# A dynamic convolution with a gated feed-forward behind it: the shifted copy of x by a second transposing DMA, scales from sums of magnitudes, and a written order for six blocks

## The chip, the cores and the metric

The kernel runs on one core of a Trainium2 chip. The metric is the time of one execution on the device in microseconds; below, "us" is always that. TensorE does the matmuls, VectorE, ScalarE and GpSimd work on tiles element by element, and the queue of SyncE issues nearly all DMAs.

## What is computed

For each of 16384 tokens (4 sequences of 4096) the reference mixes the last seven rows of x, with a softmax over seven numbers per head as weights, and puts the result through a normalised, gated feed-forward.

```python
w = softmax(weight_gen, axis=-1)                     # 8 heads, 7 taps
out = einsum('bshk,bskhg->bshg', w, x_unf)           # x_unf: the last 7 rows of x, 8 heads of 24
x = out.reshape(B * S, 192)
xn = x / sqrt(mean(x * x) + 1e-06) * rms_g
g = xn @ w_gate                                      # 192 x 1536
val = xn @ w_val
return (g * sigmoid(g) * val) @ w_out                # 1536 x 192
```

x, weight_gen and rms_g are 32-bit; the three weight matrices come as 64-bit numbers.

## The kernel before

**Blocks and stages.** A block is 512 tokens; there are 32. For each block VectorE (with TensorE for blocks 0 and 1) forms the seven taps, ScalarE and GpSimd make the factor of the norm, and the result is split in two 16-bit halves, high and low, in the tile sp. A transposing DMA turns sp into tt, with the 192 features on the partitions. Stage 1 (s1_mm) multiplies by w_gate and w_val in 12 chunks of 128 hidden columns: nine pairs of matmuls a chunk, gate on 64 partitions and value on the other 64, which run side by side. Each pair wants some 64-row groups of x on the upper and some on the lower half of the partitions, so there is a second tile tu, which is tt with its two halves swapped (PLACE says which group lies where). Products of high and low halves are summed in a bank of PSUM. s1_evac takes the two banks out (silu on ScalarE, the product on VectorE), s1_split makes the 16-bit halves of the hidden values (tile hh), stage 2 (s2_mm) multiplies by w_out and s2_evac writes the result out.

**Transposes.** The function trans issues three DMAs on SyncE's queue: the transpose sp to tt, and two copies of 64 partitions from tt to tu, which wait for the transpose to land. The same queue issues the loads of x and the weights and the writes of the result.

**Weights.** The 64-bit words of w_gate and w_val come in four slices (SL) of 2, 3, 3 and 4 chunks, loaded by load_gate_val with one DMA for the gate, to 64 partitions, and one for the value, to the other 64. decode turns them in place into 32-bit numbers (two steps on ScalarE, two on VectorE). A scale, a power of two, is found for each column and slice: ScalarE squares the slice (square_slice, tile sq), TensorE sums the squares (L524), VectorE copies the sums (L530), TensorE sums them again (L533, L538) and VectorE takes the root by arithmetic on the exponent (scales). Then high_gate_val and low_gate_val write the 16-bit halves in wm. w_out goes the same way (square_out, scale_out, tile wost). Slices 2 and 3 are kept in rawb, one of the two buffers that hold hh later.

**The order.** For blocks 0 to 3 (FRONT = 4) the order of the instructions on all five engines is written out by hand: each letter of the string START advances one stream of work by a step. W is a matmul on zeros that keeps TensorE at work (heat), A, B, C, c, D and G are the convolutions of blocks 0 to 5, s the scales, t and T the high and low halves of wm, S stage 1 in order of blocks 0 to 3, E and F its two evacuation steps, H and L the split, O stage 2. From block 4 on a planner lays the pairs of blocks out: 24 chunks of stage 1, then 24 steps of stage 2, with the convolutions of the next two blocks between them by cost.

Of the kernel before, what the change touches and what calls it, by code (L numbers as in the profile page):

```python
# [19 lines left out]
P = 128  # L20
R = 16
# [5 lines left out]
LOADS = ("w0", "x0", "s0", "w1", "x1", "s1", "s2", "s3", "x2", "wo", "w2", "x3", "x4")  # L27
START = (
    "M.....aaaa..a.aWWWWWWWWWWWWWWWWWWAAAdd!AAAb1bAbb1bd1AAAAbddBsgAB1AsBAAAAAWgsAAttjjWWgBgj"
    "gsABBjstBmmjTTTssB1mttSStTEBsTBTBmEsF1SmSBEttBFstTSBsBETTFHBHBEBs.Lt.BtSCFFBtuSTSETTHEEu"  # L30
    "L.FHSSSFECuLBLHvSvEHFFLuESSCvFEHuESFSCvLEvCFLCCyEHSEHLLyFHCHHSFyFLEzZSFEzzzCHzzSzLCZEEzF"
    "ZLZCCZSZZZzzHzLZEHSCCSEzZZOCZLCHFCCOOCOOFO3PCPECHCCCcLLOOHcQCOOOFOScFFLLPHHHHFQLcQPHESFS"
    "LLc3EFHEHLSSQESL.EEFFHH3LccFccSSS3OOEOcc3cHPO3OEccOLLQLLcDOOFOOOPcOEcSFcQDccccEcDcSHDFSE"
    "LPFDScEDDDFEDFDQHSEHHFDLLHDHFSESPSLLEFFHFLDELGSSS.EDHDEEFFDHGGDDLFSSESHEHSEQLLGLGDFSHGFG"
    "OLOOHGOGDHHHOLPGEOLFDGFOLGHDGEHOQGFOFOOOOHLHDLLPOPQQLLDPQOODOOOOOGGPGOPQGGPOQGOPGGGGQQG"
# [14 lines left out]
def tile_dynamic_conv_swiglu(  # L50
# [35 lines left out]
    p_h = ctx.enter_context(tc.tile_pool(name="p_h", bufs=2))  # L86
# [8 lines left out]
    def take():  # L95
        return banks[idle.pop(0)]
# [15 lines left out]
    eps = const.tile([P, 1], F32, name="eps")  # L112
# [83 lines left out]
    xsp = {}  # L196

    def conv(i, pe=False):
# [11 lines left out]
        if not pe and i < FRONT + 2:  # L210
# [13 lines left out]
        for k in range(K if pe or i >= FRONT + 2 else 0):  # L224
# [36 lines left out]
        if pe or i < FRONT + 2:  # L261
            sp = p_s.tile([P, J, 2 * D], F16, tag="sp", name="sp", bufs=1)
# [11 lines left out]
            xsp[i] = sp  # L274
# [15 lines left out]
        xsp[i] = sp  # L290

# [3 lines left out]
    def trans(i):  # L295
        sp = xsp.pop(i)
# [620 lines left out]
```

## Time and profile before

| | us |
|---|---|
| three runs | 1169.66, 1170.32, 1170.42; median 1170.32 |
| span of the profiled execution | 1168.1 (its own time is not listed apart) |
| TensorE busy | 1159.1 (99%) |
| VectorE, ScalarE, GpSimd busy | 938.7, 654.9, 556.6 |
| first stage-1 matmul, in the chain that ended last | 35.93 |
| end of the last matmul in that chain | 1164.78 |

The span runs from the first to the last instruction of the profiled execution; the times of the three runs are taken around the whole execution. Matmuls are pipelined, so the busy time of TensorE says that it always had one in work, not that it ran at its peak. A row of a time line gives the start, the time taken, the engine, the line of the kernel, the operation, the tiles written and read and, in brackets, how long the engine stood idle before and what ended that.

### The profile page before, as it was taken

Reading aid. Unit: us, or ns where it says so; the run is one execution under the profiler, and the core shown is the slowest. Engines: PE = TensorE matmul, PEld = TensorE weight load, DVE = VectorE, ACT = ScalarE, POOL = GpSimd, SP = SyncE. Lnnn points to the kernel's source line nnn. Section 1 sums busy time; section 2 is a strip of 40 time slices with the busy share of each in tenths; the row PEclk is TensorE's granted clock in tenths of the full one; section 3 lists DMA queues with packets and bytes.
Section 4 is the critical chain, followed back from the end, with each engine's and each line's share of the span. In section 5 each row is a group of like instructions: output and inputs, shape, how many; then the busy total and the mean of one; then the engine's idle time right before and its main releaser. Section 6 shows DMA issues by size and latency. Waiting matters only on the chain.

```text
span 1168.1 us, 24415 instructions
## 1 busy us (share of the span) xinstructions
PE 1159.1 (99%) x10182; PEld 628.7 (54%) x10183; DVE 938.7 (80%) x1120; ACT 654.9 (56%) x1275; POOL 556.6 (48%) x466
## 2 busy tenths in 40 slices
PE   8999999999999999999999999999999999999998
PEld 4455564564645546465564645546465464645546
DVE  8999976888788887888878898788987888778531
ACT  5986555556365563646636465465645646455462
POOL 1223463626365453645636456353644627355351
PEclk9999999999999999999999999999999999999999
DMA  9603322050110501114030330304102030110300
GB/s 222 182 2 116 118 42 56 1 172 1 42 42 5 168 1 45 39 36 137 2 82 1 66 107 1 82 1 135 39 19 64 2 82 2 41 42 1 82 1 28
DMA packets 67638, 67.34 MB, mean 58 GB/s; under 512 B 52428, under 2 KB 54604, under 8 KB 66632
## 3 DMA queue, kind: packets, MB, share of 16 engines
q1 hardware_dynamic: 67016, 64.77, 20.9%
q8 instruction: 79, 1.29, 0.4%
q10 hardware_dynamic: 480, 1.02, 0.4%
q14 instruction: 31, 0.25, 0.1%
q0 software_dynamic: 32, 0.00, 0.0%
HBM read 28.03 MB, written 12.58 MB: 35 GB/s over the span
## 4 chain that ended last, share of the span: by engine, by line
PE 97%; DMA 2%; ACT 0%; SPq 0%; issue 0%; ACTq 0%
PE bank L350 64%; PE bank L402 21%; PE bank L405 11%; DMA rawb<-in_moe_w_val_dram 2%; DMA rawa<-in_moe_w_gate_dram 1%; PE bank L396 0%; ACT rawb L451 0%; ACT rawb L445 0%; ACT sq L512 0%; PE bank L601 0%; PE bank L524 0%; SPq L489 0%; SPq L146 0%; ACT ot L415 0%; SPq L143 0%
## 5 line engine op out<-in xcount | busy, mean ns | idle before, releaser
L379 POOL TENSOR_TENSOR hh<-hf,hh 128x512 f16<-128x512 f32 x372 | 462.6, 1251 | 312.5 <-ACT hh L377 305.7
L350 PEld LDWEIGHTS <-wm 64*128 64x128 f16 x6912 | 334.7, 94 | 408.2 <-issue 3.8
L350 PE MATMUL bank<-tt,wm 64*128 64x512 f16 x3456 | 476.1, 376 | 0.0
L350 PE MATMUL bank<-tu,wm 64*128 64x512 f16 x3456 | 475.9, 376 | 0.0
L363 ACT ACTIVATE sg<-bank,isc 128x512 f32<-128x512 f32 x384 | 263.4, 686 | 227.9 <-PE bank L350 227.0
L402 PE MATMUL bank<-wo,hh 128*128 128x384 f16 x1524 | 374.9, 326 | 0.0
L405 PE MATMUL bank<-wo,hh 128*128 128x192 f16 x1524 | 373.4, 246 | 0.0
L367 DVE SCALAR_TENSOR_TENSOR hf<-bank,cs,sg 128x512 f32<-128x512 f32 x384 | 283.5, 744 | 111.1 <-ACT sg L363 108.8
L377 ACT ACTIVATE hh<-hf 128x512 f16<-128x512 f32 x384 | 238.1, 623 | 32.7 <-DVE hf L367 32.6
L233 DVE TENSOR_TENSOR taps<-xg,wt 128x768 f32<-128x768 f32 x170 | 233.9, 1379 | 0.0
L247 DVE TENSOR_TENSOR acc<-acc,taps 128x768 f32<-128x768 f32 x156 | 209.8, 1345 | 0.9
L402 PEld LDWEIGHTS <-hh 128*128 128x128 f16 x1524 | 149.1, 98 | 104.7 <-issue 7.2
L405 PEld LDWEIGHTS <-hh 128*128 128x128 f16 x1524 | 149.1, 98 | 0.0
L260 POOL TENSOR_TENSOR rs<-rs,mhalf 128x4 f32<-128x4 f32 x32 | 42.1, 1316 | 187.6 <-DVE rs L256 187.6
L422 DVE SCALAR_TENSOR_TENSOR ot<-bank,so,lo 128x192 f32<-128x192 f32 x127 | 51.8, 408 | 85.4 <-ACT lo L421 85.4
L421 ACT ACTIVATE lo<-bank,so 128x192 f32<-128x192 f32 x127 | 50.3, 411 | 96.4 <-PE bank L405 95.2
L252 ACT ACTIVATE junk<-acc 128x192 bf16<-128x192 f32 x120 | 43.4, 362 | 51.3 <-DVE acc L247 48.8
L287 POOL TENSOR_TENSOR sp<-xn,sp 128x768 f16<-128x768 f32 x26 | 42.8, 1645 | 53.3 <-ACT sp L285 53.3
L285 ACT ACTIVATE sp<-xn 128x768 f16<-128x768 f32 x26 | 22.0, 845 | 76.0 <-DVE xn L278 76.0
L278 DVE TENSOR_TENSOR xn<-acc,rs 128x768 f32<-128x768 f32 x26 | 24.9, 956 | 17.6 <-POOL rs L260 17.6
L233 DVE TENSOR_TENSOR acc<-xg,wt 128x768 f32<-128x768 f32 x26 | 35.4, 1360 | 0.0
L214 DVE TENSOR_TENSOR taps<-xg,wt 128x768 f32<-128x768 f32 x28 | 27.3, 995 | 0.0
(96 smaller groups left out, 304.7 us busy)
## 6 DMA issues: line engine op xcount, KB each, us to landing
tu<-tt SPq DMA_DIRECT2D x64, 192.0 KB, 3.0
out_dram<-ot SPq DMA_DIRECT2D x31, 384.0 KB, 3.0
xg<-in_x_dram SPq DMA_DIRECT2D x7, 1536.0 KB, 8.8
wt<-in_weight_gen_dram SPq DMA_DIRECT2D x7, 448.0 KB, 9.4
wost<-in_moe_w_out_dram SPq DMA_DIRECT2D x1, 2304.0 KB, 10.5
xg<-in_x_dram SPq DMA_DIRECT2D x4, 576.0 KB, 5.4
xg<-in_x_dram SPq DMA_DIRECT2D x3, 504.0 KB, 5.7
xg<-in_x_dram SPq DMA_DIRECT2D x2, 384.0 KB, 6.8
```

The costliest lines, as they stand in the source:

```text
L233: mul = nc.vector.tensor_tensor(out=dst.rearrange("p j (h c) -> p (j h) c", h=H), in0=xk, in1=wk, op=ALU.mult)
L247: yield nc.vector.tensor_tensor(out=acc, in0=acc, in1=dst, op=ALU.add)
L252: yield nc.scalar.activation(out=junk, in_=acc[:, j - a, :], func=AF.Square, accum_out=ssq[:, j : j + 1])
L350: mm = nc.tensor.matmul(pt, wm[h, grp, wpart, f], xT[i][half != m][h, q], start=(n == 0), stop=(n == 8))
L363: gate = nc.scalar.activation(out=sg, in_=pg, func=AF.Silu, scale=isc[:, o : o + 1])
L367: both = nc.vector.scalar_tensor_tensor(out=hf_of[i, c], in0=pv, scalar=cs1[:, c : c + 1], in1=sg, op0=ALU.mult, op1=ALU.mult)
L377: yield nc.scalar.activation(out=hid[i][:, 0, c, :], in_=hf, func=AF.Copy)
L379: yield low.tensor_tensor(out=hid[i][:, 1, c, :], in0=hf, in1=hid[i][:, 0, c, :], op=ALU.subtract)
L402: mm = nc.tensor.matmul(pt[:, 0 : 2 * D], hid[i][:, 0, n, c], wo[:, n, :], start=(n == 0), stop=False,)
L405: nc.tensor.matmul(pt[:, 0:D], hid[i][:, 1, n, c], wo[:, n, 0:D], start=False, stop=(n == NC - 1),)
L421: yield nc.scalar.activation(out=lo, in_=pt[:, D : 2 * D], func=AF.Identity, scale=so[:, 1:2])
L422: nc.vector.scalar_tensor_tensor(out=ot[i][:, t, :], in0=pt[:, 0:D], scalar=so[:, 1:2], in1=lo, op0=ALU.mult, op1=ALU.add,)
```

## The change

- The tile sp becomes a part of a wider tile, spare, with 64 zero columns ahead of it and behind it. trans issues two transposing DMAs from it: tt from the middle part, and tu from the whole tile, which shifts the groups by 64 columns, so that each group lies on the other half of the partitions. tu has 13 blocks where tt has 12. The two copies and PLACE are gone; xpart_of finds a group's place.
- The scales come from sums of magnitudes. After the first of decode's two VectorE steps the lower half of each 64-bit word holds the magnitude; its upper 16 bits, every fourth half word of the tile, are read by TensorE as weights (sizes). The squares on ScalarE are gone, and the first sum is squared when it is taken out (ScalarE, six to eight columns). A small constant (least) is added by one more matmul a chunk.
- Stage 1, stage 2, their evacuations and the split have a stream each for even and for odd blocks, the order is written for blocks 0 to 5, and the string of LOADS and steps is new. hh becomes two fixed tiles, hids, one for even and one for odd blocks. Slice 2 is kept in wo until w_out needs it, slice 3 in the upper half of hids[1]. LOW_BY says for each split of the six blocks whether VectorE ("v") or GpSimd ("p") makes the low half.
- The first load of weight_gen goes by SyncE's queue, and w1 is issued ahead of x0.

```diff
-DECODE = ("aa",) * (3 * NS + 4)
-FRONT = 4
+LOW_BY = "ppppppppppppppvvppvpvvpvpvvpppvppppv", "pppppppppvppvvppvpppppvpvvppppvvvpvp"
+FRONT = 6
+LEAD = 6
...
+    SPAN = J * 6 * L
+    spare = const.tile([P, SPAN + 2 * L], F16, name="spare")
+    spl = spare[:, L : L + SPAN].rearrange("p (j c) -> p j c", j=J)
+    hids = [const.tile([P, NC, 2, TB], F16, name=f"hid{n}") for n in range(2)]
...
-        (nc.scalar if a == g == 0 else nc.sync).dma_start(out=dst[:, a:b, :], in_=src[:, a:b, :])
+        nc.sync.dma_start(out=dst[:, a:b, :], in_=src[:, a:b, :])
...
         tt = p_t.tile([P, J * 3, P], F16, tag="tt", name="tt")
-        nc.sync.dma_start_transpose(out=tt, in_=sp.rearrange("p j c -> p (j c)"))
-        tu = p_t.tile([P, J * 3, P], F16, tag="tu", name="tu")
-        nc.sync.dma_start(out=tu[L:P], in_=tt[0:L])
-        nc.sync.dma_start(out=tu[0:L], in_=tt[L:P])
-        xT[i] = [t.rearrange("p (j q) c -> p q j c", q=3) for t in (tt, tu)]
+        nc.sync.dma_start_transpose(out=tt, in_=spare[:, L : L + SPAN])
+        tu = p_t.tile([P, J * 3 + 1, P], F16, tag="tu", name="tu")
+        nc.sync.dma_start_transpose(out=tu, in_=spare)
+        xT[i] = tt, tu
+
+    def xpart_of(i, h, blk, part):
+        t, u = xT[i]
+        b = 3 * part + blk
+        if b % 2 == h:
+            t, q = t, b // 2
+        else:
+            t, q = u, (b + 1) // 2
+        return t[h * L : (h + 1) * L, q : q + 3 * (J - 1) + 1 : 3, :]
...
-    def square_slice(k):
-        n = (SL[k][1] - SL[k][0]) * P
+    def decode_slice(k):
         yield from decode(raws[k].rearrange("p m f -> p (m f)"), "aa")
-        sqs[k] = p_d.tile([P, 3, 4 * P], BF16, tag="sq", name="sq", bufs=2)
-        whole = upper(raws[k].rearrange("p m f -> p (m f)")).bitcast(F32)
-        yield nc.scalar.activation(
-            out=sqs[k][:, :, 0:n], in_=whole.rearrange("p (m f) -> p m f", m=3), func=AF.Square, bias=eps,
-        )
+
+    def sizes(raw):
+        return raw.bitcast(BF16).rearrange("p (f t) -> p f t", t=4)[:, :, 1]
...
                 nc.tensor.matmul(
-                    pt[:, 3 + 2 * c : 5 + 2 * c], sq[:, m, c * P : (c + 1) * P], g2[:, m, :],
-                    start=(m == 0), stop=(m == 2),
-                )
+                    pt[:, 3 + 2 * c : 5 + 2 * c], sizes(raws[k][:, m, c * P : (c + 1) * P]), g2[:, m, :],
+                    start=(m == 0), stop=False,
+                )
+            nc.tensor.matmul(pt[:, 3 + 2 * c : 5 + 2 * c], ones[0:1, :], least, start=False, stop=True)
...
-        nc.vector.tensor_copy(out=sums[:, 0 : w - 3], in_=pt[:, 3:w])
+        nc.scalar.activation(out=sums[:, 0 : w - 3], in_=pt[:, 3:w], func=AF.Square, scale=2.0**-12)
...
+    half = [[(i, c) for i in range(n, FRONT, 2) for c in range(NC)] for n in range(2)]
+    for n in range(2):
+        streams["SV"[n]] = each((s1_mm, i, c) for i, c in half[n])
+        streams["Oo"[n]] = each((s2_mm, b, *unit(u)) for b in range(n, FRONT, 2) for u in range(NC))
```

How the string moves the instructions on ScalarE, ahead of the first stage-1 evacuation (sg), before: rawb holds slices 2 and 3 (1536 columns are slice 3), sq the squares, junk is block 1's norm.

```order
L445 ACTIVATE rawb<-rawb 128x1152
L451 ACTIVATE rawb<-rawb 128x1152
L512 ACTIVATE sq<-rawa,eps 128x3x384
L562 ACTIVATE wm<-rawa,gs 128x256
L445 ACTIVATE rawb<-rawb 128x1536
L451 ACTIVATE rawb<-rawb 128x1536
L512 ACTIVATE sq<-rawb,eps 128x3x384
L252 ACTIVATE junk,ssq<-bank_93 128x192
L562 ACTIVATE wm<-rawa,gs 128x384 x3
L363 ACT_TABLE_LOAD
```

And the same place on ScalarE with the change: wo holds slice 2, hid slice 3, sums are the squared sums of slices 1 and 2.

```order
L421 ACTIVATE wo<-wo 128x1152
L427 ACTIVATE wo<-wo 128x1152
L492 ACTIVATE sums<-bank_92 128x6
L421 ACTIVATE hid_116<-hid_116 128x1536
L427 ACTIVATE hid_116<-hid_116 128x1536
L492 ACTIVATE sums<-bank_91 128x6
L524 ACTIVATE wm<-rawa,gs 128x256
L524 ACTIVATE wm<-rawa,gs 128x384 x2
L255 ACTIVATE junk,ssq<-bank_89 128x192
L524 ACTIVATE wm<-rawa,gs 128x384
```

The squares are gone, two steps of six columns stand for them, and the two decodes of slice 3 stand ahead of the second of these and of the last high half of slice 0.

On SyncE's queue, from the last two loads of weights on, before: the transposes and copies of blocks 0 and 1, the rest of x (128x1536), w_out and the next weight_gen.

```order
L489 DMA rawb<-in_moe_w_gate_dram 64x3x512
L489 DMA rawb<-in_moe_w_val_dram 64x3x512
L299 DMA_TRANSPOSE tt<-sp 128x12x128
L302 DMA tu<-tt 64x1536
L303 DMA tu<-tt 64x1536
L168 DMA xg<-in_x_dram 128x1536
L578 DMA wost<-in_moe_w_out_dram 128x12x192
L175 DMA wt<-in_weight_gen_dram 128x896
L299 DMA_TRANSPOSE tt<-sp 128x12x128
```

The same place on SyncE's queue with the change, up to block 1's transposes and the loads behind them.

```order
L468 DMA hid_116<-in_moe_w_gate_dram 64x3x512
L468 DMA hid_116<-in_moe_w_val_dram 64x3x512
L298 DMA_TRANSPOSE tt<-spare 128x12x128
L301 DMA_TRANSPOSE tu<-spare 128x13x128
L540 DMA wost<-in_moe_w_out_dram 128x12x192
L298 DMA_TRANSPOSE tt<-spare 128x12x128
L301 DMA_TRANSPOSE tu<-spare 128x13x128
L173 DMA xg<-in_x_dram 128x1536
L180 DMA wt<-in_weight_gen_dram 128x896
```

Each block has two DMAs here in place of three, none of them waits for the one ahead of it to land, and block 1's now stand ahead of the rest of x.

## Rows read from the trace of the kernel before

**Rows 1.** The page: busy time, share of the span and instructions by engine.

```profile
PE 1159.1 (99%) x10182; PEld 628.7 (54%) x10183; DVE 938.7 (80%) x1120; ACT 654.9 (56%) x1275; POOL 556.6 (48%) x466
```

**Rows 2.** Chain that ended last, first 50 us: start, us, what.

```profile
11.62 19.40 DMA rawb<-in_moe_w_val_dram
...
32.67 1.63 ACT rawb L451
34.29 1.22 ACT sq L512
...
35.93 3.99 PE bank L350 x36
...
40.23 3.99 PE bank L350 x36
44.23 0.39 PE bank L524 x12
```

**Rows 3.** The same chain over the whole span.

```profile
68.52 1.17 PE bank L601 x24
...
179.77 46.73 PE bank L350 x432
...
250.12 46.73 PE bank L350 x432
...
1164.78 0.42 ACT ot L415
```

**Rows 4.** Time line of ScalarE (ACT): a step of three columns, slice 3's first decode.

```profile
13.60 0.17 ACT L660 ACTIVATE g_sb<-bank 128x3 f32<-128x3 f32 x1 [0.88 <-PE bank L656]
...
31.11 1.68 ACT L445 ACTIVATE rawb<-rawb 128x1536 f32<-128x1536 f32 x1 [1.05 <-DMA rawb<-in_moe_w_val_dram]
```

**Rows 5.** Time line of TensorE (PE): taps of blocks 0 and 1, heating matmuls.

```profile
13.49 5.43 PE L240 MATMUL bank<-taps,ident 128*128 128x384 f32 x16
...
24.35 0.59 PE L788 MATMUL bank<-dull 128*128 128x512 bf16 x2
27.02 2.93 PE L240 MATMUL bank<-taps,ident 128*128 128x384 f32 x4 [2.08 <-DVE taps L233]
```

**Rows 6.** Groups of TensorE's weight loads (PEld) by form: busy us, mean ns.

```profile
L240 PEld LDWEIGHTS bank<-taps,ident 128*128 128x128 f32 x56 | 10.5, 199 | 11.1 <-DVE taps L233 3.9 <-issue 2.1
```

**Rows 7.** Time line of SyncE's queue (SPq): transposes and first copies, blocks 0 and 1.

```profile
24.89 1.53 SPq L299 DMA_TRANSPOSE tt<-sp  x1
32.52 0.53 SPq L302 DMA_DIRECT2D tu<-tt  x1
...
50.67 1.43 SPq L299 DMA_TRANSPOSE tt<-sp  x1
54.34 0.47 SPq L302 DMA_DIRECT2D tu<-tt  x1
```

**Rows 8.** Stretches of block 1's transpose and copies: busy us by engine, PEclk, DMA share, GB/s.

```profile
51.50:54.00 2.50, 2.50 (x26) 1.17 (x24) 2.50 (x5) 2.50 (x6) 1.29 (x1) 1.00 0.83 157
55.00:57.50 2.50, 2.50 (x26) 1.15 (x24) 2.50 (x4) 2.50 (x4) 0.85 (x1) 1.00 0.63 155
```

**Rows 9.** DMA issues: the row of gains, size, us from issue to landing.

```profile
g_row<-in_moe_rms_g_dram POOLq DMA_DIRECT2D x1, 0.8 KB, 7.0
```

**Rows 10.** Time line of GpSimd (POOL): the issue of that DMA.

```profile
2.14 0.68 POOL L650 DMA_DIRECT2D g_row<-in_moe_rms_g_dram  x1
```

**Rows 11.** Stretches of the start: busy us of PE, PEld, DVE, ACT, POOL, then PEclk.

```profile
25.00:30.00 5.00, 2.98 (x12) 1.47 (x13) 5.00 (x5) 4.46 (x5) 0.00 (x0) 0.70 1.05 205
...
50.00:55.00 5.00, 5.00 (x50) 2.26 (x48) 5.00 (x9) 5.00 (x8) 1.77 (x2) 1.00 0.42 80
```

**Rows 12.** Groups of VectorE (DVE) by form, 50 to 180 us: busy us, mean ns.

```profile
L367 DVE SCALAR_TENSOR_TENSOR hf<-bank,cs,sg 128x512 f32<-128x512 f32 x44 | 32.2, 746 | 4.2 <-ACT sg L363 2.9 <-POOL hh L379 1.3
L220 DVE TENSOR_REDUCE acc<-taps 128x192 f32<-128x1344 f32 x16 | 24.3, 1545 | 0.1
L379 DVE TENSOR_TENSOR hh<-hf,hh 128x512 f16<-128x512 f32 x12 | 8.4, 699 | 0.0
```

More of the change, by code (lines that the diff above doesn't have):

```diff
@@ L111, in tile_dynamic_conv_swiglu @@
     g_sb = const.tile([P, 3], F32, name="g_sb")
-    eps = const.tile([P, 1], F32, name="eps")
+    least = const.tile([1, 2], BF16, name="least")
     ones = const.tile([P, P], BF16, name="ones")
@@ L209, in conv @@
             parts = ((0, J, acc),)
-        if not pe and i < FRONT + 2:
+        if not pe and i < LEAD:
             prod = taps.rearrange("p k n -> p (k n)").rearrange("p (j d k e) -> p j d k e", j=J, k=K, e=2)
@@ L223, in conv @@
                 )
-        for k in range(K if pe or i >= FRONT + 2 else 0):
+        for k in range(K if pe or i >= LEAD else 0):
             if k or pe:
@@ L373, in s1_split @@
     def s1_split(i, c):
[L374 to L375 removed]
+        hid = hids[i % 2]
         hf = hf_of.pop((i, c))
[L377 to L378 removed]
+        yield nc.scalar.activation(out=hid[:, c, 0, :], in_=hf, func=AF.Copy)
+        low = nc.vector if i < FRONT and LOW_BY[i % 2][NC * (i // 2) + c] == "v" else nc.gpsimd
         yield low.tensor_tensor(
[L380 removed]
+            out=hid[:, c, 1, :], in0=hf, in1=hid[:, c, 0, :], op=ALU.subtract
         )
@@ L464, in decode, with scales @@
         )
-    def scales(v, s, r, e):
-        nc.vector.tensor_scalar(
-            out=s.bitcast(I32), in0=v.bitcast(I32), scalar1=-0.5, scalar2=205.5 * 2.0**23,
-            op0=ALU.mult, op1=ALU.add,
-        )
+    def scales(v, s, r, e, n):
+        for a, b, root, top in ((0, n, -0.5, 205.5), (n, v.shape[1], -1.0, 270.0)):
+            if a < b:
+                nc.vector.tensor_scalar(
+                    out=s[:, a:b].bitcast(I32), in0=v[:, a:b].bitcast(I32), scalar1=root, scalar2=top * 2.0**23,
+                    op0=ALU.mult, op1=ALU.add,
+                )
         nc.vector.tensor_single_scalar(
@@ L606, in scale_out @@
         sums = p_d.tile([P, 2 * 4], BF16, tag="sums", name="sums", bufs=2)
-        nc.vector.tensor_copy(out=sums[0:half, 0:2], in_=pt[0:half, 0:2])
+        nc.scalar.activation(out=sums[0:half, 0:2], in_=pt[0:half, 0:2], func=AF.Square)
         for u in range(2):
@@ L639, in tile_dynamic_conv_swiglu @@
     nc.gpsimd.tensor_copy(out=ident16, in_=ident32)
-    nc.gpsimd.memset(eps, EPS)
+    nc.gpsimd.memset(spare[:, 0:L], 0.0)
+    nc.gpsimd.memset(spare[:, L + SPAN :], 0.0)
+    nc.gpsimd.memset(least, 2.0**-40)
     nc.gpsimd.memset(ones, 1.0)
-    nc.gpsimd.memset(part[:, 0, :], 2.0**-23)
+    nc.gpsimd.memset(part[:, 0, :], 1.0)
     nc.gpsimd.memset(part[:, 1:3, :], 0.0)
@@ L777, in conv_trans @@
         yield from conv(i, pe)
-        if i in BY_PE:
-            yield from trans_pe(i)
-        else:
-            yield trans(i)
-    dull = const.tile([P, TB], BF16, name="dull")
+        yield trans(i)
+    dull = hids[0][:, 0, 0, :]
     def heat():
@@ L790, in heat @@
             yield mm
-    both = [(i, c) for i in range(FRONT) for c in range(NC)]
+    half = [[(i, c) for i in range(n, FRONT, 2) for c in range(NC)] for n in range(2)]
     streams = {
@@ L835, in tile_dynamic_conv_swiglu @@
             go(ch)
-    assert not left and all(next(gen, 0) == 0 for ch, gen in streams.items() if ch not in "MW")
+    assert not loads and all(next(gen, 0) == 0 for ch, gen in streams.items() if ch not in "MW")
     pend = []
```

153 lines of the change are left out of this document (48 added, 105 removed).

## The prediction

> **What bounds the kernel now.** First the busy line: TensorE is busy 1159.1 of 1168.1 us [rows 1]. That is no proof, since a busy TensorE is not one at its peak, so next I looked for idle in the chain that ended last. From 35.93 us, when the first stage-1 matmul starts, the chain never leaves TensorE until 1164.78 [rows 2, 3]. A pair of blocks takes 250.12 - 179.77 = 70.35 us; sixteen pairs are 1125.6 of the 1128.9 us between, and the rest is the small matmuls for the scales that stand among them (0.31 us between 39.92, where the piece that starts at 35.93 ends, and 40.23; 0.39 at 44.23; 1.17 at 68.52). So the time is three pieces: 35.9 us until stage 1 starts, 1128.9 us without a gap, and 3.3 us of tail. The change leaves the stage-1 and stage-2 matmuls and the tail as they are. It can gain only by an earlier start or fewer small matmuls, and lose by any new gap. The 0.2% that a measurement of this kernel can tell from no change is 2.3 us, so faster needs a start near 33.5.
>
> What sets the start before? The chain goes back through TensorE's sums of slice 2, ScalarE's square of that slice (34.29), its two decodes of slice 3 (31.11, 32.67) and the landing of slice 3's value half, issued at 11.62 and 19.40 us under way [rows 2]. ScalarE stood 1.05 us waiting for that landing [rows 4].
>
> **The change part by part.** *Magnitudes for squares.* In ScalarE's new order the two decodes of slice 3 (128x1536) still stand ahead of the sums of slice 2, on which TensorE's last step before stage 1 waits. The bytes issued ahead of slice 3 are the same: loads w0, x0, s0, w1, x1, s1, s2, only with w1 ahead of x0, and all of slice 3 is issued long before its turn. I keep its landing at 31.0. Then 31.11 + 1.56 + 1.62 (from start to start, as 31.11, 32.67, 34.29) puts the decodes' end at 34.2. The square of 1.22 is gone from here; in its place is a square of six columns, nearest row 0.17 [rows 4]: 34.4. TensorE then does the nine small matmuls of slice 2's second sum, 0.31 as measured, and one heating matmul (0.59 for two, so 0.30 [rows 5]): stage 1 starts at about 35.1 instead of 35.93, **0.8 us gained**. Those nine matmuls no longer stand inside stage 1 (0.3 gained), but slices 3 and w_out get matmuls whose weights are every fourth half word of the raw tile, and one more matmul per chunk (least): four at 0.39/12 = 0.03, so 0.1 lost, if strided weights load as packed ones do. **Net -1.0 us.**
>
> No row shows a strided weight load. Bounds: 0.03 to 0.05 us each as the packed ones (0.39 for 12, 1.17 for 24 [rows 2, 3]), and 0.20 each as an fp32 weight load, which reads four bytes an element [rows 6]. On the path are 12 + 24 of them: 0 to +5.6 us (12 x 0.17 + 24 x 0.15). I take the low end, because the element and its type are those of the packed rows. [...]
>
> *Swapped tile by a second transpose.* Before, the queue issued one transpose and two copies; the copies waited for the transpose to land (24.89 to 32.52 for block 0, behind the weights; 50.67 to 54.34 for block 1, 3.7 us [rows 7]). Now a second transpose follows the first. The first's packets keep the DMA engines busy 0.83 of 2.5 us, 2.1 us; the copies 0.63 of 2.5, 1.6 us [rows 8]. With 13 blocks for 12 the second takes 2.2: it lands about 2.2 us after the first, so 5.9 after the first's issue, where the copies ended about 7 after. [...] From block 2 on both have many microseconds to spare. For block 1 the new order has stage 1 start after eight chunks of block 0, 8 x 1.95 + 0.9 of small matmuls = 16.5 after the start, at 51.6 (46.73/24 = 1.95 a chunk [rows 3]). VectorE has 22 instructions between slice 0's last low, at 35.2, and block 1's last; at the trace's durations of their shapes they are 11.3 us, so with 0.4 of waiting for ScalarE, an estimate, that one ends at 46.9. The first transpose lands at 50.6, the second at 52.8; stage 1 wants it after four of nine pairs, at 52.5. I put **+0.3 us** there.
>
> *The start of block 0.* The gains now stand ahead of block 0's taps on TensorE, so its row of gains, landing 7.0 us after an issue at 2.14 [rows 9, 10], plus 0.2 for two more memsets ahead on GpSimd, holds the taps until 9.3; with gains and two heating matmuls they start at about 10.5. Fourteen matmuls are 28 records at 5.43/16 = 0.34: 20.0, against 18.92 before (13.49 + 5.43) [rows 5]. TensorE stands idle some 2.5 us ahead of them, and after an idle of 2.08 before (24.94 to 27.02) the granted clock was 0.70 in 25 to 30, half of the taps' pace gone (2.93 for four records) [rows 5, 11]: that cost 0.30 x 5 = 1.5 us of TensorE work, and here up to 2: taps end at 20 to 22. Before, the transpose was issued 6.0 after them; now one more decode (1.2, three quarters of slice 3's) is in ScalarE's way: 7.2 to 7.5, so issue at 27.5 to 29.5. ScalarE reaches slice 3's decode 8.7 after the taps, 28.7 to 30.7, still ahead of 31.1. The transposes land behind the weights at 32.5 and 35 at the latest, and stage 1 wants the second at 36.0. **Cost 0**, covered by the landing of slice 3; with that cover gone it is 1 to 3 us.
>
> *Order for six blocks.* Before the first stage-2 matmul both orders have 23 chunks of stage 1 to feed. VectorE's queue for them has 76 rows before and 74 after: six splits of 0.70 and some casts less, three products of 0.75, one reduction of 1.55 and two softmax steps more [rows 12], equal within half a microsecond. VectorE was fully busy there, 5.00 of 5.00, and TensorE had no idle [rows 11]. ScalarE loses its squares. With steps of equal weight I take **0**, up to +2 if a wait of one engine for another falls badly. Sum: 1168.1 - 1.0 + 0.3 = 1167.4. The median of the three runs is 2.2 above the span; carried over, 1169.6. I write 1169.8 for small waits.
>
> **The rivals.** *Clock low at the first stage-1 matmul* (0.27). After block 1's last tap (about 32) TensorE has only the small sums, two heating matmuls and a wait for ScalarE until 35.1, much like the stretch before 27.02. [...] Against it: taps may run later than I think and fill the stretch. *Slice 3 is not waited for* (0.11): if the new order of loads lands it 1.5 us or more earlier, ScalarE is the limit: 30.7 or 28.7 + 3.2 + 0.8 = 34.7 or 32.7, so 1169.2 down to 1167.2. For it: two halves of slice 0 run on two queues; against: the same bytes. *Strided weight loads cost their bound* (0.11), the slower side: 36 loads on TensorE between the chunks of slice 3 and w_out at 0.20 give +5.6, 1175.4; it decides from about 0.12 each, +2.9. *Order with waits* (0.10): block 1's or 2's second transpose late, or an engine's queue held by another, 2 to 4 us: 1171.8 to 1174.
>
> **How the numbers follow.** Forecast 0.41, 1169.8, itself 1168.9 to 1170.8. Faster by over 0.2% is below 1168.0: the better half of the second rival, 0.07, and a tail of the forecast, 0.04: 0.11. Slower is above 1172.7: strided loads 0.08, waits 0.06, and the low clock with small waits on top 0.04, 0.18. The rest, 0.71, is no change. For 8 in 10 I leave out what is below 1167.8 and above 1173.0.
>
> **What would show it.** The first stage-1 matmul at 35.1 (34 to 36), released through ScalarE's two decodes of slice 3, whose first waits for a DMA that lands near 31; no wait of TensorE after it but some tenths at block 1's first chunk; pairs of 70.35 us. The small sums of w_out near 1.2 us, not 4.8. Wrong would be: a start near 33, a granted clock under 1 after it, or gaps among the chunks of blocks 0 to 5.

## The result, and the profile after

The changed kernel takes 1186.83 us (median of four runs, 1185.36 to 1188.31), the kernel before 1170.37 beside it (four runs): a ratio of 1.0144, 95% interval 1.0129 to 1.0158. The forecast was 1169.8, no change. The profiled execution has a span of 1184.9 us, 16.8 more than the 1168.1 of before.

Two pieces of the page: the busy row of TensorE, and the shares of the chain that ended last, by engine.

```profile
PE 1169.7 (99%) x10195; PEld 637.9 (54%) x10195; DVE 953.2 (80%) x1128; ACT 646.2 (55%) x1274; POOL 552.7 (47%) x459
...
PE 90%; DVE 2%; ACT 1%; issue 1%; DMA 0%; POOL 0%; DVEq 0%; POOLq 0%; ACTq 0%
```

TensorE is "99% busy" as before, and that again says little. But its share of the chain is 90%, where the page of before has 97%, and VectorE is in it, which in the chain before [rows 2, 3] it is not. The same chain in order of time (start, us, what) shows where:

```profile
66.00 0.67 DVE hf L343
...
70.05 2.25 PE bank L556 x24
72.30 3.75 PE bank L327 x18
...
90.27 1.72 DVE wo L580 x2
91.99 1.89 DVE spare L270 x3
...
103.57 2.15 DVE wo L580 x2
...
142.07 4.16 DMA tu<-spare
...
266.99 46.73 PE bank L327 x432
...
337.34 46.73 PE bank L327 x432
...
1178.64 2.98 PE bank L372 x36
1181.65 0.42 ACT ot L391
```

From 245 us on nothing is lost: a pair of blocks takes 337.34 - 266.99 = 70.35 us, as before [rows 3], and the tail is 1184.9 - 1181.6 = 3.3, as before. All 16.8 us lie ahead of block 6. What TensorE waited for, with the sum, the count and the longest:

```profile
PE bank L612 <- DMA g_row<-in_moe_rms_g_dram: 4.6, 1, 4.6
PE bank L378 <- DVE wo L580: 2.1, 3, 0.9
PE bank L748 <- DVE hid L782: 1.2, 1, 1.2
PE bank L327 <- DVE hf L343: 1.1, 2, 0.6
PE bank L381 <- DVE hid L354: 0.9, 1, 0.9
PE bank L327 <- ACT sg L339: 0.9, 1, 0.9
PE bank L495 <- ACT sums L492: 0.8, 1, 0.8
PE bank L327 <- DMA tu<-spare: 0.3, 1, 0.3
```

The waits for g_row, for the sums and of the heating matmuls (L748) stand ahead of stage 1; the others make 5.3 us, a third of the loss. This view misses the rest, so I went through TensorE's records from the first stage-1 matmul on. I cut the work into pieces: the 18 matmuls of a chunk of stage 1, and 12 matmuls of stage 2 (a step and a half). Undisturbed, the next piece starts 1.942 or 1.470 us later (24 and 16 of them, with a tenth where the kind changes, are the 46.73 and 23.62 us of a pair of blocks). What a piece takes beyond that is a loss. In the kernel before it comes almost only from its small sums and its 38 changes of kind (a stretch of small sums counts as one change). What the other kernels lose beyond the kernel before falls into five kinds (us, each from one profiled execution):

| | after | lows set to zero, blocks 0 and 1 | lows set to zero, blocks 0 to 5 | both parts, old order |
|---|---|---|---|---|
| first stage-1 matmul later than 35.87 | 0.77 | 1.00 | 1.39 | -0.06 |
| changes of kind: 71 for 38 (last column 38) | 3.43 | 3.39 | 3.37 | 0.01 |
| small sums among the pieces | 1.57 | 1.58 | 1.58 | 1.88 |
| granted clock low in one piece | 1.70 | 1.48 | 1.68 | 0 |
| other waits | 9.26 | 3.34 | 0.44 | 0 |
| sum | 16.73 | 10.79 | 8.46 | 1.83 |
| span less 1168.1 | 16.8 | 10.9 | 8.6 | 1.8 |

The other columns are experiments told below. So four causes were to be tested: why TensorE waits (9.26), what a change of stage costs (3.43), what the sums cost (1.57 and the clock), and whether the second transposing DMA has any part.

**Why it waits.** VectorE works without a break here: 10.00 of 10.00 us between 60 and 70, and 20.00 of 20.00 between 80 and 100. A row has the stretch, its length, then the busy us (and instructions) of TensorE, of its weight loads, of VectorE, of ScalarE and of GpSimd:

```profile
60.00:70.00 10.00, 8.49 (x73) 3.76 (x69) 10.00 (x10) 6.09 (x13) 5.62 (x4) 1.00 0.00 0
80.00:100.00 20.00, 18.40 (x155) 10.03 (x153) 20.00 (x28) 14.03 (x35) 10.33 (x9) 1.00 0.22 42
```

Its instructions have become longer. Mean ns stands behind the busy time; first two forms of the kernel before, then the same two of the changed one:

```profile
L267 DVE SCALAR_TENSOR_TENSOR sp<-acc,rs,sp 128x192 f16<-128x192 f32 x16 | 6.9, 466 | 0.7 <-ACT sp L265 0.7
L625 DVE SCALAR_TENSOR_TENSOR wo<-wost,ws,wo 128x192 f16<-128x192 f32 x12 | 4.3, 410 | 0.0
```

```profile
L270 DVE SCALAR_TENSOR_TENSOR spare<-acc,rs,spare 128x192 f16<-128x192 f32 x16 | 12.4, 801 | 0.0
L580 DVE SCALAR_TENSOR_TENSOR wo<-wost,ws,wo 128x192 f16<-128x192 f32 x12 | 8.0, 713 | 0.0
```

The time lines of VectorE and GpSimd in the changed kernel, 88 to 95 us, show when:

```profile
88.43 0.68 DVE L270 SCALAR_TENSOR_TENSOR spare<-acc,rs,spare 128x192 f16<-128x192 f32 x1
89.03 2.96 DVE L580 SCALAR_TENSOR_TENSOR wo<-wost,ws,wo 128x192 f16<-128x192 f32 x3
91.92 1.97 DVE L270 SCALAR_TENSOR_TENSOR spare<-acc,rs,spare 128x192 f16<-128x192 f32 x3
93.80 1.35 DVE L438 SCALAR_TENSOR_TENSOR wost<-wost 128x1152 int32<-128x1152 int32 x1
95.07 1.06 DVE L580 SCALAR_TENSOR_TENSOR wo<-wost,ws,wo 128x192 f16<-128x192 f32 x3
```

```profile
87.74 2.40 POOL L354 TENSOR_TENSOR hid<-hf,hid 128x512 f16<-128x512 f32 x2 [0.44 <-ACT hid L352]
90.30 1.15 POOL L354 TENSOR_TENSOR hid<-hf,hid 128x512 f16<-128x512 f32 x1 [0.16 <-ACT hid L352]
92.31 1.35 POOL L354 TENSOR_TENSOR hid<-hf,hid 128x512 f16<-128x512 f32 x1 [0.87 <-ACT hid L352]
```

Three L580 take 1.06 from 95.07, with GpSimd idle, and 2.96 from 89.03, beside its lows. Of the six, two of L580 and one of L270 are long, and in the records each of these ends 0.2 us after a low of GpSimd: 90.34 behind 90.14, 91.66 behind 91.45, 93.88 behind 93.67. An instruction that began just ahead of a low kept its own time (L270 at 92.25, the low from 92.31), and there the low took 1.35 us where the shortest take 1.15. Over the whole trace the L270 that read acc take a median of 0.40 us where GpSimd's two-operand work doesn't overlap them and 1.27 where it does, the low on VectorE (L354) 0.68 and 1.10 (overlaps of a quarter of a us or more), the sum of taps (L250) 0.95 and 1.71. The evacuation L343 takes 0.74 either way: of its two tile operands one is in PSUM. This looked like VectorE and GpSimd shutting each other out where VectorE reads two SBUF operands. Adding up what VectorE's instructions between 36 and 110 us take beyond the shortest of their form (evacuations left out) gives 1.0 us before and 12.0 after. What moved is GpSimd's work: the lows of blocks 0 and 1, of which every second was on VectorE before, are on GpSimd but for one, and its two-operand instructions take 37.6 us of that stretch for 22.1.

### The profile page after: what moved, and what is told of

The parts are those of the page before. It is cut to its first block, busy times and chain, and to the rows that moved or that the text cites. A ratio compares the mean times of both kernels' runs of the same rounds, so it can differ in the third digit from the quotient of the medians.

```text
span 1184.9 us, 24383 instructions
## 1 busy us (share of the span) xinstructions
PE 1169.7 (99%) x10195; PEld 637.9 (54%) x10195; DVE 953.2 (80%) x1128; ACT 646.2 (55%) x1274; POOL 552.7 (47%) x459
## 4 chain that ended last, share of the span: by engine, by line
PE 90%; DVE 2%; ACT 1%; issue 1%; DMA 0%; POOL 0%; DVEq 0%; POOLq 0%; ACTq 0%
PE bank L327 58%; PE bank L378 21%; PE bank L381 10%; DVE hf L343 1%; DVE spare L270 0%; ACT sg L339 0%; DVE wo L580 0%; DMA tu<-spare 0%; ACT hid L352 0%; PE bank L372 0%; ACT wo L575 0%; ACT junk L255 0%; PE bank L556 0%; DVE taps L236 0%; DVE acc L250 0%
## 5 line engine op out<-in xcount | busy, mean ns | idle before, releaser
L354 POOL TENSOR_TENSOR hid<-hf,hid 128x512 f16<-128x512 f32 x363 | 454.0, 1258 | 342.9 <-ACT hid L352 334.3
L327 PEld LDWEIGHTS <-wm 64*128 64x128 f16 x6912 | 341.6, 94 | 406.8 <-issue 15.6
L378 PE MATMUL bank<-wo,hid 128*128 128x384 f16 x1524 | 377.3, 326 | 2.2 <-DVE wo L580 2.1
L381 PE MATMUL bank<-wo,hid 128*128 128x192 f16 x1524 | 373.4, 246 | 0.9 <-DVE hid L354 0.9
L343 DVE SCALAR_TENSOR_TENSOR hf<-bank,cs,sg 128x512 f32<-128x512 f32 x384 | 282.9, 742 | 111.2 <-ACT sg L339 108.5
L352 ACT ACTIVATE hid<-hf 128x512 f16<-128x512 f32 x384 | 237.1, 622 | 45.0 <-DVE hf L343 41.3
L378 PEld LDWEIGHTS <-hid 128*128 128x128 f16 x1524 | 149.0, 98 | 110.6 <-issue 14.4
L250 DVE TENSOR_TENSOR acc<-acc,taps 128x768 f32<-128x768 f32 x156 | 206.7, 1325 | 0.8
L381 PEld LDWEIGHTS <-hid 128*128 128x128 f16 x1524 | 149.1, 98 | 4.4 <-POOL hid L354 2.0
L263 POOL TENSOR_TENSOR rs<-rs,mhalf 128x4 f32<-128x4 f32 x32 | 40.8, 1275 | 181.4 <-DVE rs L259 169.4
L289 POOL TENSOR_TENSOR spare<-xn,spare 128x768 f16<-128x768 f32 x26 | 42.9, 1650 | 57.3 <-ACT spare L287 57.3
L287 ACT ACTIVATE spare<-xn 128x768 f16<-128x768 f32 x26 | 21.9, 842 | 71.0 <-DVE xn L280 71.0
```

The costliest lines, as they stand in the source:

```text
L250: yield nc.vector.tensor_tensor(out=acc, in0=acc, in1=dst, op=ALU.add)
L327: mm = nc.tensor.matmul(pt, wm[h, grp, wpart, f], xpart_of(i, m, grp, xpart), start=(n == 0), stop=(n == 8))
L343: both = nc.vector.scalar_tensor_tensor(out=hf_of[i, c], in0=pv, scalar=cs1[:, c : c + 1], in1=sg, op0=ALU.mult, op1=ALU.mult)
L352: yield nc.scalar.activation(out=hid[:, c, 0, :], in_=hf, func=AF.Copy)
L354: yield low.tensor_tensor(out=hid[:, c, 1, :], in0=hf, in1=hid[:, c, 0, :], op=ALU.subtract)
L378: mm = nc.tensor.matmul(pt[:, 0 : 2 * D], hid[:, n, 0, c], wo[:, n, :], start=(n == 0), stop=False,)
```

## The experiments

**Each part alone, in the order of before.** The second transposing DMA:

```diff
-        nc.sync.dma_start_transpose(out=tt, in_=sp.rearrange("p j c -> p (j c)"))
+        nc.sync.dma_start_transpose(out=tt, in_=spare[:, L : L + SPAN])
...
-        nc.sync.dma_start(out=tu[L:P], in_=tt[0:L])
-        nc.sync.dma_start(out=tu[0:L], in_=tt[L:P])
...
+        nc.sync.dma_start_transpose(out=tu, in_=spare)
...
```

> The kernel before with one edit, the second transposing DMA in place of the two copies (and, to make room for its larger tile, the heating matmuls read a tile of 128 columns four times instead of one of 512). The two parts together, in the order of before, came to 1171.9, the magnitudes alone to 1173.0, of which 1.6 was one fall of the granted clock; so this edit is worth 0 within 1 us: 1169.7 to 1171.2, no wait of TensorE for the swapped tile. If the order is not the cause and the transposes are, 3 us or more above.

With the heating tile as it was, the output's tiles want 7.5 KB a partition where 6.84 are left.

1169.85 us (ten runs), ratio 0.9999 [0.9989, 1.0008]. TensorE's waits, all ahead of stage 1, name no transposed tile:

```profile
PE bank L243 <- DVE taps L236: 4.3, 4, 2.1
PE bank L534 <- ACT sq L522: 2.0, 3, 1.2
PE bank L801 <- DVE dull L839: 1.0, 1, 1.0
```

The transposes cost nothing that ten runs can tell (from 1.3 us less to 0.9 more). The changed kernel's one wait for tu (0.3 us, 4.16 of DMA in the chain at 142 us) is a consequence: it is gone in the last of the runs with lows set to zero.

The magnitudes:

```diff
-                    pt[:, 3 + 2 * c : 5 + 2 * c], sq[:, m, c * P : (c + 1) * P], g2[:, m, :],
-                    start=(m == 0), stop=(m == 2),
+                    pt[:, 3 + 2 * c : 5 + 2 * c], sizes(raws[k][:, m, c * P : (c + 1) * P]), g2[:, m, :],
+                    start=(m == 0), stop=False,
...
+            nc.tensor.matmul(pt[:, 3 + 2 * c : 5 + 2 * c], ones[0:1, :], least, start=False, stop=True)
...
```

> The kernel before with one edit: the weight scales from sums of magnitudes, read by TensorE as every fourth half word of the raw tiles; the squares go out of ScalarE's queue and everything else keeps its place in the order. In the changed kernel the sums of slice 3 took 1.19 us for 0.39 and those of w_out 2.25 for 1.17. If these prices are the weight loads' own, they come back here, 0.8 + 1.1 = 1.9 us, less at most 0.8 for an earlier start: 1171.5 to 1172.5. My forecast's term for this part was -1.0, so 1169.4. If the sums were dear only because the new order put them beside something else, 1169.4 to 1170.4.

1173.03 us, 1.002 [1.001, 1.003], half a microsecond above the range that I gave; the small sums cost 1.88 us more, as expected, and the clock fell behind them in the profiled run (1.62). The start was 0.3 earlier, less than starts differ between kernels with the same start (35.3 to 37.1, below).

Both together:

> The kernel before with both edits together, the second transposing DMA and the magnitudes, in the order of before: the changed kernel without its new order, its table of lows and its shared tiles. If the order is what costs, this is the sum of the two alone, 1170.4 to 1173, and some 14 us below the changed kernel's 1186.8. If the loss came from the two parts meeting (the raw tiles kept longer, the transposes later), this is above the sum by 3 us or more.

1171.92 us, 1.0018 [1.0008, 1.0027], 14.9 below the changed kernel, and the last column of the table: nothing but the sums. The rest comes with what this kernel lacks: the new order with its table of lows and its loads, and the shared tiles.

**A change of stage.**

```diff
                     pend.append((i, c))
+                    if i == a + 1 and c == 7:
+                        for u in range(3):
+                            s2_mm(a, *unit(u))
+                        run(s2_evac(a, 0))
...
```

> The kernel before with one edit in its steady loop: of each of 14 pairs of blocks, three pieces of stage 2 of the first block are moved up between two pieces of stage 1 of the second. So TensorE goes from stage 1 (64-row matmuls) to stage 2 (128-row) and back once more per pair, 28 changes more, with the same matmuls. In the trace of before a piece of stage 1 ahead of a change takes 2.04 us for 1.94 and a piece of stage 2 ahead of one 1.56 for 1.47. If that tenth is the price of a change, this costs 28 x 0.096 = 2.7 us: 1173.1. If the tenth is an artefact of how ends are modelled or hidden elsewhere, 1170.4. The changed kernel has 71 changes for 38, so the first reading puts 3.2 to 3.4 of its 16.8 us here.

1180.16 us, 1.0081 [1.0066, 1.0097]: 9 us, where I expected 2.7. The account of the pieces parts it: 28 changes more cost 2.76 us, 0.099 each, as expected; the start of this run was 1.0 later; and 6.2 are waits that I hadn't foreseen, six times a long one in the steady loop:

```profile
PE bank L350 <- DVE ot L422: 4.0, 6, 0.7
```

The early step of stage 2 holds a bank of PSUM until VectorE takes it out, and stage 1 wants that bank. The price of a change holds; the run also shows that what is moved brings its banks along.

**The lows on GpSimd.** First the choice of the changed kernel put into the kernel before:

```diff
-        low = nc.vector if i < 2 and c % 2 else nc.gpsimd
+        low = nc.vector if (i, c) == (1, 9) else nc.gpsimd
```

> The kernel before with one edit: the low halves of blocks 0 and 1 go to GpSimd, all but one, as in the changed kernel, where before had every second on VectorE. Same order on all engines otherwise; VectorE has 11 instructions of 0.69 us less. Theory: VectorE and GpSimd shut each other out when VectorE's instruction reads two SBUF operands, since in the changed kernel the low of the normalized x takes 0.40 us with GpSimd idle and 1.20 beside its low, 0.95 becomes 1.71 for the sums of taps, and the evacuations from PSUM stay at 0.74. Then VectorE's instructions of blocks 0 to 2 that read two SBUF operands get longer here too, by some 8 to 15 us in all, and eat the 7.6 us saved: 1170.4 to 1178. By rival (the lengthening comes from the transposes or the shared tiles of the changed kernel) their durations stay as before and the time is 1170.4.

1171.52 us, 1.0012 [1.0002, 1.0021]. VectorE has 7.6 us less to do between 36 and 110 us and gets 7.2 of it back by longer instructions (8.2 for 1.0 by the sum above). So moving eleven instructions off the busiest engine bought nothing, and in the profiled execution (1173.77 us, among the longest of the ten) TensorE waits 2.7 us where it had not. Two forms of VectorE, 1.36 and 0.75 long before:

```profile
L459 DVE SCALAR_TENSOR_TENSOR wost<-wost 128x1152 int32<-128x1152 int32 x2 | 4.7, 2332 | 0.0
...
L569 DVE SCALAR_TENSOR_TENSOR wm<-rawb,gs,wm 128x512 f16<-128x512 f32 x3 | 3.7, 1300 | 0.0
```

There is no second transposing DMA and no shared tile in this kernel, so the lengthening comes from GpSimd's lows alone. Then the choice of before put into the changed kernel:

```diff
-LOW_BY = "ppppppppppppppvvppvpvvpvpvvpppvppppv", "pppppppppvppvvppvpppppvpvvppppvvvpvp"
+LOW_BY = "pvpvpvpvpvpvppvvppvpvvpvpvvpppvppppv", "pvpvpvpvpvpvvvppvpppppvpvvppppvvvpvp"
```

> The changed kernel with one edit: in blocks 0 and 1 every second low half goes back to VectorE, as before; order unchanged. Theory of the two engines shutting each other out: VectorE gets 11 x 0.68 = 7.5 us more work and loses about half of the 15.7 us by which its instructions are longer than before between 34 and 260 us; with less in GpSimd's queue too, 1182 to 1187. Rival (VectorE simply has too much to do in this order): 7 us slower, 1190 to 1194.

1188.13 us against 1186.83: neither theory's numbers. The lengthening falls from 12.0 to 6.0 us and VectorE has 7.5 more to do; TensorE's waits are 10.3 for 9.3. Of the rest, the start was 2.1 later in this run and no clock fell behind the sums. In this order VectorE is too full either way, and the table of lows can't mend it.

So the cause was taken away instead. The lows of blocks 0 and 1 by ScalarE:

```diff
+        if i < 2 and low is nc.gpsimd:
+            yield nc.scalar.activation(out=hid[:, c, 1, :], in_=hf, func=AF.Copy, scale=2.0**-12)
+            return
```

> The changed kernel, order unchanged, with the 23 low halves of blocks 0 and 1 that GpSimd made written by ScalarE instead, as a plain scaled copy of 0.62 us that reads the same tile and sets the same tile free (the low half itself is left out, so the output is not the reference's). GpSimd is idle then through most of blocks 0 and 1. Theory: VectorE's instructions fall back to their own durations there, and of TensorE's waits between 63 and 107 us (6.2 us in seven places and 1.7 of lowered clock after them) most vanish: 1178 to 1182. Rival (the order itself starves TensorE): 1185 or more. ScalarE's added 14 us may cost up to 2 us where it was full, before 60 us.

1184.04 us: only 2.8 less. VectorE's lengthening is gone (0.6 us), but ScalarE can't take the load: TensorE now waits 2.0 us for its sg. Inconclusive by itself. The lows as sets by GpSimd, which leaves the low halves out as well:

```diff
+        if i < 2 and low is nc.gpsimd:
+            yield low.memset(hid[:, c, 1, :], 0.0)
+            return
```

> The same as the run with ScalarE, but GpSimd keeps the 23 instructions and sets the low halves to zero (a write with no read; the low half is left out). GpSimd's queue and order stay, each instruction is shorter (a set of 256 columns took 0.34 us before) and reads nothing. Theory: what shuts VectorE out is GpSimd's reading, so its instructions keep their own durations beside these: 1177 to 1181. [...] If any GpSimd work lengthens VectorE's, beside these sets they are still 0.3 to 0.6 us longer.

1180.94 us, 5.9 less, and the second column of the table: TensorE's waits fall by 5.9 us, those ahead of 107 us from 6.1 to 0.3. VectorE and GpSimd in the stretch that was shown above:

```profile
86.30 0.41 DVE L270 SCALAR_TENSOR_TENSOR spare<-acc,rs,spare 128x192 f16<-128x192 f32 x1
86.62 1.07 DVE L583 SCALAR_TENSOR_TENSOR wo<-wost,ws,wo 128x192 f16<-128x192 f32 x3
87.62 1.06 DVE L270 SCALAR_TENSOR_TENSOR spare<-acc,rs,spare 128x192 f16<-128x192 f32 x3
```

```profile
85.12 4.25 POOL L355 MEMSET hid<- 128x512 f16 x9
```

GpSimd works through all of it (85.12 to 89.37), and VectorE's instructions keep their 0.4 us. So it isn't GpSimd's being busy that shuts VectorE out; of what its lows do and its sets don't, the reading is left. L270 takes 0.41 us beside sets here, and 1.27 (median) beside lows in the changed kernel.

The same for blocks 0 to 5 (i < FRONT in the edit above):

> The changed kernel, order unchanged, with every low half that GpSimd makes in blocks 0 to 5 set to zero by GpSimd (written, not read; the low halves are left out). With those of blocks 0 and 1 alone it took 1180.9, and TensorE's waits left behind 107 us were 3.5 us in ten places (0.6 of them for a swapped tile at 139). Theory: the ones at 168 to 179 and at 234 come from VectorE's instructions lengthened by GpSimd's lows of blocks 2 to 5, so they go: 2.3 us less, 1178 to 1179. What is left over the kernel before is then 3.3 for more changes between stage 1 and 2, 1.6 for small sums, 1.5 for a fall of the clock behind them and the start. Rival (these waits come from the order itself): 1181.

1178.24 us, as expected. TensorE's waits, complete:

```profile
PE bank L615 <- DMA g_row<-in_moe_rms_g_dram: 4.2, 1, 4.2
PE bank L751 <- DVE hid L785: 1.2, 1, 1.2
```

Both stand ahead of stage 1. Of the 9.26 us of waits 0.44 are left, all on engines other than a transposing DMA. With that the waits are shown to come from GpSimd's lows in this order. One thing is not parted: a set takes 0.47 us (4.25 for nine) and a low 1.15 or more, so GpSimd's own queue is shorter in these two runs too. In the changed kernel, up to 260 us, VectorE waits for a low of GpSimd only twice, 1.7 us in all, and its instructions in the stretch from 36 to 110 us alone are 12.0 us longer; so the lengthening is much the larger share, but that is argued from the trace. A run with the true lows and without their overlap would need another order and wasn't made.

**The sums.** The step of the weight loads alone: the squares of before, read with a step of four (the scales are only near the right ones):

```diff
-                    pt[:, 3 + 2 * c : 5 + 2 * c], sq[:, m, c * P : (c + 1) * P], g2[:, m, :],
+                    pt[:, 3 + 2 * c : 5 + 2 * c],
+                    sq[:, m, c : 4 * P : 4] if k == 3 else sq[:, m, c * P : (c + 1) * P], g2[:, m, :],
...
-                    pt[0:half, u : u + 1], sqw[c // HC][:, c % HC, u * half : (u + 1) * half], ih2[:, c : c + 1],
+                    pt[0:half, u : u + 1],
+                    sqw[c // HC].rearrange("p c d -> p (c d)").rearrange(
+                        "p (b n t) -> p b n t", n=half, t=4)[:, c % 3, :, 2 * u + c // 3 % 2],
+                    ih2[:, c : c + 1],
```

> The kernel before with one edit: the squares of slice 3 and of w_out stay where they are, but TensorE loads them as weights with a step of four half words instead of packed (the same 12 + 24 matmuls and the same squares, other columns together, so the scales are only near the reference's). No matmul is added. In the magnitudes' kernels a strided weight load came to 0.06 us of 128 columns and 0.094 of 96, for 0.033 and 0.049 packed. If the step is the price: slice 3 0.39 -> 0.76, w_out 1.17 -> 2.25, together 1.45 us, so 1171.6, and 1173.2 if the granted clock falls behind the sums of w_out as it did in five of the seven profiles with magnitudes. My forecast took 0 for the step: 1170.2.

1173.77 us, 1.0023 [1.0013, 1.0033]. The median holds more than the price of the sums: in six of the ten runs the clock fell too (mean granted clock 0.995 and 1173.7 to 1174.4 us, against 1.0 and 1170.0 to 1171.7). So the prices are read from the profiled execution (1170.98), where no clock fell. W_out's sums in it:

```profile
68.52 2.32 PE L602 MATMUL bank<-ih,sq 128*96 128x1 bf16 x24
70.77 1.25 PE L350 MATMUL bank<-tt,wm 64*128 64x512 f16 x9
```

70.77 - 68.52 = 2.25 us for 24, where packed ones take 1.17 [rows 3]: 0.094 for 0.049 each. But slice 3's twelve loads of 128 columns took 0.49 for 0.39, 0.041 each for 0.033. So of the 0.80 that slice 3 costs in the changed kernel only 0.10 is the step; the 0.70 that is left I put on the four matmuls of least, whose weights are one row: 0.17 each, an estimate from these two runs. No run has these alone.

Does the fall of the clock behind the sums, 1.5 to 1.7 us in the profiles that have it, belong to so many small matmuls, or to strided weight loads? The sums of w_out made twice, packed:

```diff
-        for u in range(2):
+        for u in (0, 0, 1, 1):
             for c in range(NC):
```

> The kernel before with one edit: the 24 matmuls of w_out's sums are made twice over, packed as before, so TensorE spends 2.34 us on two-column matmuls between two pieces of stage 1 and not 1.17. [...] If it belongs to strided weight loads, the clock stays and the time is 1171.4.

1172.28 us, 1.0019 [1.0010, 1.0028], between 1171.4, which the 1.17 us of more sums make alone, and the 1173.0 that they make with a fall of the clock on top. In its profile the clock fell:

```profile
67.92 2.32 PE L601 MATMUL bank<-ih,sq 128*96 128x1 bf16 x48
70.17 2.13 PE L350 MATMUL bank<-tt,wm 64*128 64x512 f16 x9
71.67 2.30 PE L350 MATMUL bank<-tu,wm 64*128 64x512 f16 x9
```

Stage 1's nine matmuls take 2.13 and 2.30 for 1.25, without a wait and without a strided load: 1.68 us. In the changed kernel the same stands in the view by windows (the granted clock is the 0.72, behind the engines' busy times):

```profile
70.00:75.00 5.00, 5.00 (x39) 3.66 (x40) 5.00 (x6) 1.32 (x3) 2.62 (x2) 0.72 0.01 3
```

Microsecond by microsecond from 72 to 76 the granted clock there is 0.62, 0.50, 0.50 and 0.67: half speed for 3.4 us, which loses 1.7. So the fall, which I first put down to TensorE's waits, came behind some 2.3 us of one-column matmuls, strided or packed; it came in five of the seven profiles with magnitudes, also where TensorE had not waited at all before (with the lows of blocks 0 to 5 set to zero, the groups of nine behind the sums take 2.11 and 2.32 for 1.25). Why not in all seven, nor in the profile with strided squares, isn't settled.

**The start.** A last run tried to win some tenths for the kernel before. Its runs beside the experiments lie in two groups: 33 of the 34 with a mean granted clock of 1.0 take 1169.2 to 1170.5 us, the 29 with 0.997 take 1170.7 to 1172.1. Its profiled execution (0.998) has the granted clock at half from 26.99 to 30.40, behind an idle stretch of 2.08 us on TensorE:

```diff
-    "M.....aaaa..a.aWWWWWWWWWWWWWWWWWWAAAdd!AAAb1bAbb1bd1AAAAbddBsgAB1AsBAAAAAWgsAAttjjWWgBgj"
+    "M.....aaaa..a.aWWWWWWWWWWWWWWWWWWAAAdd!AAAb1bAbb1bd1AAAAbddBsgAB1AsBAAAAAWgsAAttjjWWWWWWWWgBgj"
```

> The kernel before with one edit: six heating matmuls of 512 columns more where TensorE stands idle for 2.08 us (24.94 to 27.02) ahead of block 1's first taps. [...] If the fall there is what parts the groups, the extra matmuls take it away and all runs lie at 1169.2 to 1170.2, median 0.3 to 0.8 below that of before. If the fall comes at the start whatever TensorE does in that gap, or costs nothing because ScalarE sets the start, no difference.

1170.49 us against 1170.0, 1.0005 [0.9996, 1.0014]. The mean granted clock was 0.999 or 1.0 in all eleven runs, and nothing was gained: ScalarE's first decode of slice 3 still waited for its landing, 1.74 us, and started at 31.71. No run points to a version that beats the kernel before.

## Why the prediction was wrong, step by step

- **Bound, pairs and tail:** right. 70.35 us a pair, 3.3 of tail, all else in the front.
- **"Stage 1 starts at about 35.1":** the chain was right, the size not. ScalarE again waits for slice 3 (1.98 us), but its decode starts at 32.86, not 31.1; the two decodes and the square of six columns take 3.2 as put down, and TensorE starts at 36.64. "I keep its landing at 31.0" failed, by 1.75: the value half of slice 3 was issued at 11.59, as before (11.62 [rows 2]), but took 21.2 us to land where it had taken 19.4. With an untouched start the kernels in the order of before began stage 1 between 35.3 and 37.1, those in the new order between 36.4 and 38.8. The decode of slice 3 parts the two more clearly: it began between 30.6 and 31.7 in all nine profiles of the old order and between 32.3 and 33.9 in all five of the new one, so at least part of the delay belongs to the new order. Why the load takes longer there wasn't tested. First the load (KB, us from issue to landing), then ScalarE's time line:

```profile
hid<-in_moe_w_val_dram SPq DMA_DIRECT2D x1, 768.0 KB, 21.2
```

```profile
32.86 1.68 ACT L421 ACTIVATE hid<-hid 128x1536 f32<-128x1536 f32 x1 [1.98 <-DMA hid<-in_moe_w_val_dram]
34.43 1.58 ACT L427 ACTIVATE hid<-hid 128x1536 int32<-128x1536 uint32 x1
35.90 0.15 ACT L492 ACTIVATE sums<-bank 128x6 bf16<-128x6 f32 x1
```

- **"if strided weights load as packed ones do":** they don't, for 96 columns. The net of -0.2 for the small matmuls (0.3 gained, 0.1 lost) was +1.57: -0.31 of slice 2 as put down, +0.80 for slice 3 and +1.08 for w_out. The bounds of 0 to +5.6 held it, the chosen end did not: the element and its type, for which I took it, don't tell the price, since in the run with strided squares the same step costs 0.008 at 128 columns and 0.045 at 96. What parts the two, no run shows. "Four at 0.39/12 = 0.03" for the added matmuls was 0.17 each, by the estimate above. And behind 2.25 us of small matmuls the granted clock fell to half for 3.4 us, which cost 1.7 us; I looked for that only at the start.
- **+0.3 for block 1's second transpose; "From block 2 on both have many microseconds to spare":** right but for one place. The second transpose alone measured -0.3 (interval -1.3 to +0.9), and no piece between 50 and 61 us lost anything, where block 1 comes in. At 142 us a later block's tu was 0.3 us late, which the order had brought about.
- **"Cost 0" for the start of block 0:** right. The transposes were issued at 29.47 and 31.10, no matmul of stage 1 waited for them there, and the landing of slice 3 covered the rest.
- **"With steps of equal weight I take 0":** the step that failed, by 12.7 us. I counted VectorE's queue (76 and 74 rows) and multiplied by durations from the trace of before. The "six splits of 0.70 [...] less" were not saved: they and five more went to GpSimd, and there they lengthened what VectorE did beside them, by 12.0 us for 1.0 between 36 and 110 us. The 0.70 of a low [rows 12], and the durations of other forms with two SBUF operands, didn't hold beside GpSimd's two-operand work: a low took 1.10 there, L270 1.27 for 0.40. Before's own trace would have told it, where the sum of taps takes 0.96 alone and 1.71 beside GpSimd (medians). Nor did I count the changes of stage, 71 for 38, although the order shows them and the trace of before the tenth that each costs: 3.4 us. With the start (1.6), the small matmuls (1.8) and the clock (1.7) and without the 0.3 for block 1 this is the way from the 1167.4 of the sum to the span of 1184.9. (The 2.2 us between span and time were 1.8 in the profiled execution, 1186.71 less 1184.9.)
- **The rivals:** "order with waits" was the right kind, but with 2 to 4 us sized for one late tile or one held queue, and given 0.10. It was 9.3 of waits in some twenty places. "Strided weight loads cost their bound" is decided at 0.12 each and measured 0.04 to 0.09, so it fell: 1.2 of its 5.6 us came. "Clock low at the first stage-1 matmul" fell: the granted clock is 1.00 from 35 to 40 us. "Slice 3 is not waited for" fell: ScalarE waited 1.98 us for it.
- **What would show it:** "gaps among the chunks of blocks 0 to 5" and "a granted clock under 1" after the start were named as signs of a wrong forecast, and the trace has both.

## What to carry to other kernels

Before taking durations from one order into another, look at what ran beside them: split each form by whether GpSimd was reading at the time, and cost a step moved to GpSimd by what it does to VectorE, not by what it saves there. When an order is rewritten, count the changes between kinds of matmul as well as the matmuls. A gapless bound engine hides how little slack the engine behind it has: here moving 7.6 us of work off VectorE, in the old order, already made TensorE wait, 2.7 us in the profiled execution.

## What the runs showed of the hardware

- In the changed kernel VectorE instructions with two SBUF operands that started while a wide two-operand instruction of GpSimd ran were held: medians of 1.27 for 0.40 (L270) and 1.71 for 0.95 (L250); the short ones looked at ended some 0.2 us after GpSimd's. (Beside GpSimd's power of four columns, L263, an L580 kept its 0.40.) L343 with one operand in PSUM took 0.74 either way and the reduction of one operand, L223, 1.54, and beside GpSimd's sets L270 took 0.41. Two SBUF operands are not the whole condition, though: one form with a single SBUF operand, L194 with 128 columns, took 0.21 us alone (two of the seven) and 1.65 beside GpSimd (the other five, all in the steady loop, where no matmul waits for it):

```profile
409.09 1.65 DVE L194 TENSOR_SCALAR sm<-sm 128x128 f32<-128x128 f32 x1
...
409.02 1.64 POOL L289 TENSOR_TENSOR spare<-xn,spare 128x768 f16<-128x768 f32 x1 [2.39 <-ACT spare L287]
```

- TensorE lost 0.096 us at each change between 64-row and 128-row matmuls in the kernel before (3.65 us in 38 changes) and 0.099 in the run with more of them (2.76 in 28 more), and, an estimate by what is left of slice 3's sums, 0.17 for a one-row matmul among 128-row ones.
- A small matmul whose weights are loaded with a step of four half words took 0.041 us for 128 columns (0.033 packed) and 0.094 for 96 (0.049 packed).
- A second transposing DMA that makes a tile of 13 blocks did as well as two copies of 64 partitions behind the first transpose: 1169.85 us against 1170.16, ratio 0.9989 to 1.0008.
